# Moving the second tile of three pairs in the second DFT of an FNet block

## The chip, the cores and the metric

The kernel runs on one core of a Trainium2 chip. The metric is device time in microseconds (us) of one execution; lower is better. TensorE (PE) multiplies matrices into PSUM, VectorE (DVE) and ScalarE (ACT) do the elementwise work, GpSimd (POOL) a little of it, and SyncE (SP) issues all DMAs. Each engine runs its own instructions in the order in which they are written.

## The reference

```python
# x: 2048 x 448 (S x D), Df = 1792, all fp32
a = einsum("sd,ed->se", layernorm(x), dft_hid_re)
b = einsum("sd,ed->se", layernorm(x), dft_hid_im)
h = x + dft_seq_re @ a - dft_seq_im @ b            # FNet mixing
n = layernorm(h)
out = h + (gelu(n @ w_gate) * (n @ w_up)) @ w_down # GeGLU
```

## The kernel before, in words

Each fp32 operand is split into a high and a low fp16 part (`hi_part` on ACT, `lo_part` on DVE), and a product is three fp16 matmuls, so every tile of weights costs ACT and DVE work before PE can use it.

The kernel does the DFT along the sequence first, with x normalized ("first DFT", accumulators `acc` and `acc_f`), then the DFT along the hidden dimension (the "second DFT", accumulator `y`). After them comes the GeGLU in two parts (products `pX`, `pY`, `pZ`, then `acc_d`). The written order is the schedule: nothing reorders instructions, and code that is written later runs later on its engine.

The first DFT runs in 64 steps, n = 0 to 63 (`N_STEPS`). Steps 0 to 15 make the first four row tiles at once, steps 16 to 39 take 24 matmuls each, and from step 40 on (`FAST`) a Strassen scheme takes 42 narrower matmuls a step. Four such steps make a quad (40 to 43, 44 to 47 and so on), which shares four PSUM banks and ends with `fast_out`: DVE adds up the seven products (`e`) and splits the result into `zs`.

A Strassen step n needs "unit" n: the raw matrix `wr` (two DMAs, L421), its sums (`fast_sums`, DVE, L460 to L462), the high parts (ACT, L108: raw 128x768, sums twice 128x512) and the low parts (DVE, L114: 128x768 and 128x1024). From unit 43 on, a unit is written two steps before its use: unit 46 in step 44, 47 in 45, 48 in 46; units 45 and 49 stand between the matmuls of steps 43 and 47, together with `fast_out`. Three units fit in the ring `ws`, so ACT can start a unit when PE is done with the one three steps earlier. The load of `wr` for unit n can start when the low part of unit n-3's raw matrix is done.

Two row tiles (g = 0 and 1) make a pair p. For each pair, SP transposes `zs` into `z` (`z_turn`, L658, four DMAs; `z` has one buffer). For each tile of the pair, `hid_seed` (ACT, L700) puts x into the bank `y`, `hid_mm` adds 21 matmuls (PE, L719), and `hid_out` (ACT, L708 to L710) writes h and its moments from the bank. The bank `y` has a single buffer (tag `tr`), so the second tile's seed is written right behind the first tile's `hid_out`. `h_store` (SP, L733) writes the pair's h to memory; `ffn_rstd` makes the reciprocal deviation (one ACT instruction, L129, and five small DVE instructions, L140 to L144).

Two tables place this work: `early` (written after the units of step n) and `after` (written after the first or the second half of step n's matmuls, `(n, 0)` or `(n, 1)`). The first tile of pairs 0 to 6 stands at `(m, 0)`:

```python
m = (19, 24, 29, 36, 44, 52, 60)[p]
```

The fourth to sixth pair are p = 3, 4 and 5. In steps 42 to 44, ACT and DVE also normalize and split the h of p = 3 for the GeGLU (`xn_h`, `tt`, `xs`; `ffn_norm_act`, `ffn_sums`, `ffn_split`); the split stands in step 44 ahead of the `hid_out` of p = 4's first tile.

Of the kernel before, what the change touches and what calls it, by code (L numbers as in the profile page):

```python
# [32 lines left out]
def kernel(  # L33
# [92 lines left out]
    def root(mv, tag, of=1.0):  # L126
        n = mv.shape[1]
        sd = small.tile([P, n], F32, tag=f"sd{n}", name=f"sd_{tag}")
        A.activation(sd, mv[:, :, 1], AF.Sqrt, scale=1.0 / (of * X_SC**2), bias=eps_t)  # L129
        return sd  # L130
# [5 lines left out]
    def rstd(mv, sd, tag, pool=small, of=1.0):  # L136

        n = sd.shape[1]
        r = pool.tile([P, 4, n], F32, tag=f"r{n}" if pool is small else f"r_{tag}", name=f"r_{tag}")
        V.reciprocal(r[:, 0], sd)  # L140
        V.tensor_scalar(r[:, 1], mv[:, :, 1], of * EPS, -0.5 / (of * X_SC**2), op0=ALU.add, op1=ALU.mult)
        V.tensor_mul(r[:, 2], r[:, 0], r[:, 0])
        V.tensor_mul(r[:, 2], r[:, 2], r[:, 1])
        V.scalar_tensor_tensor(r[:, 3], r[:, 2], 1.5, r[:, 0], op0=ALU.add, op1=ALU.mult)  # L144
        return r[:, 3]
# [22 lines left out]
    def pair_tile(name, k):  # L168
        return ring.tile([P, 2, D], F32, tag=f"xh{k}", bufs=1, name=name)
# [28 lines left out]
    def ffn_rstd(q, j):  # L198
        tag = f"h{q}_{j}"
        mv = moments[q, j]  # L200
        moments[q, j] = mv, rstd(mv, root(mv, tag, D), tag, const, D)
# [18 lines left out]
    def ffn_bias(q, j):  # L220
        mv, r = moments[q, j]
        sign = -1.0 if (q, j) == (NB - 1, 1) else 1.0
        V.scalar_tensor_tensor(mv[:, :, 1], mv[:, :, 0], sign, r, op0=ALU.mult, op1=ALU.mult)

    def ffn_norm_act(q, j, h):

        tag = f"h{q}_{j}"
        mv, r = moments.pop((q, j))
        nb = mv[:, :, 1]
        xn = fops.tile([P, 2, D], F32, tag="xn", name=f"xn_{tag}")  # L230
        for g in range(2):
            A.activation(xn[:, g, :], h[:, g, :], AF.Identity, scale=r[:, g : g + 1], bias=nb[:, g : g + 1])
        ffn[q, j] = xn

    def ffn_sums(q, j, parts=range(4)):

        if 0 in parts:
            t = fops.tile([P, 960], F32, tag="tt", name=f"tt_{q}_{j}")
            ffn[q, j] = ffn[q, j], t
        xn, t = ffn[q, j][:2]  # L240
        sub = V.tensor_sub
        if 0 in parts:
            sub(t[:, 0:256], xn[:, 1, 0:256], xn[:, 0, 0:256])
        if 1 in parts:
            sub(t[:, 256:448], xn[:, 1, 256:448], t[:, 0:192])
            V.tensor_scalar(t[:, 448:512], t[:, 192:256], -1.0, None, op0=ALU.mult)
        if 2 in parts:
            sub(t[:, 512:704], xn[:, 1, 256:448], xn[:, 1, 0:192])
            V.tensor_scalar(t[:, 704:768], xn[:, 1, 192:256], -1.0, None, op0=ALU.mult)
        if 3 in parts:  # L250

            sub(t[:, 768:960], xn[:, 0, 256:448], t[:, 256:448])
# [31 lines left out]
    def ffn_split(q, j):  # L284
        ffn_hi(q, j)
        ffn_lo(q, j)

    def ffn_transpose(q, j, parts):
        xs = ffn[q, j][2]
        ops = hops[q if q > 1 else 0]  # L290
        c = (2 * q + j if q < 2 else j) * P
        for n in parts:
            s0, s1 = ((0, 8), (8, 16), (16, 22), (22, 25))[n]
            nc.sync.dma_start_transpose(ops[:, s0:s1, c : c + P], xs[:, s0 * P : s1 * P])
# [110 lines left out]
    N_STEPS = NT + 8 * (NP - 2)  # L405
    wr, ws = {}, {}

    def step_of(n):

        k, qq = divmod(n - NT, 4)  # L410
        return 2 + k // 2, k % 2, qq
# [242 lines left out]
    def z_turn(p):  # L654
        z[p] = hidp.tile([P, 2, 7, 2 * P], F16, tag="z", name=f"z{p}")
        for g in range(2):
            for l in range(2):
                nc.sync.dma_start_transpose(z[p][:, l, :, g * P : (g + 1) * P], zs[p][:, g, l, :])  # L658
# [32 lines left out]
    def h_tile(q, j):  # L691
        hp[q, j] = pair_tile(f"hx{q}_{j}", 2 * (q - 2) + j if q > 1 else j)
        nc.sync.dma_start(hp[q, j], xr[q // 2, 2 * (q % 2) + j])
# [3 lines left out]
    def hid_seed(p, g):  # L697

        y = ys[p, g] = ps_tr.tile([P, 512], F32, tag="tr", name=f"y_{p}_{g}")
        A.activation(y[:, :D], hp[p // 2, p % 2][:, g, :], AF.Copy, scale=D_SC)  # L700

    def hid_out(p, g):

        q, j = divmod(p, 2)
        if g == 0:
            moments[q, j] = const.tile([P, 2, 2], F32, tag=f"mv_h{q}_{j}", name=f"mv_h{q}_{j}")
        y, h, mv = ys[p, g][:, :D], hp[q, j][:, g, :], moments[q, j]
        A.activation(h, y, AF.Copy, scale=1.0 / D_SC, accum_out=mv[:, g, 0:1])  # L708
        A.activation(mv[:, g, 0:1], mv[:, g, 0:1], AF.Copy, scale=-1.0 / D)
        A.activation(y, y, AF.Square, scale=1.0 / D_SC, bias=mv[:, g, 0:1], accum_out=mv[:, g, 1:2])  # L710

    def hid_mm(p, g):

        if p == NP - 1:
            ys[p, g] = bank_tile("a3" if g else "tr", f"y_{p}_{g}")
        y = ys[p, g]
        for k in range(7):
            for m, (lz, lw) in enumerate(((0, 0), (0, 1), (1, 0))):
                PE.matmul(  # L719
                    y[:, :D],  # L720
                    z[p][:, lz, k, g * P : (g + 1) * P],
                    wh[:, lw, k, :],
                    start=p == NP - 1 and k == 0 and m == 0,
                    stop=k == 6 and m == 2,
                    skip_group_check=True,
                )
# [5 lines left out]
    def h_store(q, j):  # L732
        nc.sync.dma_start(h_dram[2 * q + j], hp[q, j])  # L733
# [6 lines left out]
    early, after = {}, {}  # L740

    def at(where, n, *what):
        where.setdefault(n, []).extend(what)
# [22 lines left out]
    for p, (n, half) in enumerate(turns):  # L766
        b, j = divmod(p, 2)
        m = (19, 24, 29, 36, 44, 52, 60)[p]
        at(early, m - 4, lambda b=b, j=j: h_tile(b, j))
        at(early, m - 2, lambda p=p: hid_seed(p, 0))  # L770
        for g in range(2):

            at(after, (m + g, int(p >= 3 and g)), lambda p=p, g=g: hid_mm(p, g), lambda p=p, g=g: hid_out(p, g))
            if g == 0:
                at(after, (m, 0), lambda p=p: hid_seed(p, 1))
        at(after, (n, half), lambda p=p: z_turn(p))
        at(early, m + 2 if p < 5 else N_STEPS - 7 + p, lambda b=b, j=j: ffn_rstd(b, j))
        at(after, (m + 2, 0), lambda b=b, j=j: h_store(b, j))
        if b < 2:

            m += 4 if p == 3 else 0
            at(early, m + 2, lambda b=b, j=j: ffn_bias(b, j), lambda b=b, j=j: ffn_norm_act(b, j, hp[b, j]))
            at(early, m + 3, lambda b=b, j=j: ffn_sums(b, j))
            at(early, m + 4, lambda b=b, j=j: ffn_split(b, j))
            for k in range(4):
                at(after, (m + 5 + k // 2, k % 2), lambda b=b, j=j, k=k: ffn_transpose(b, j, (k,)))
# [46 lines left out]
    for n in range(N_STEPS):  # L833
# [41 lines left out]
        if n >= FAST:  # L875

            last = n % 4 == 3
# [34 lines left out]
        else:  # L912
            p, part, qq = step_of(n)
# [381 lines left out]
    def bank_tile(tag, name):  # L1295
        return ps_ff[tag].tile([P, 512], F32, tag=tag, name=name)
# [102 lines left out]
    for t in range(NF, N_GU):  # L1399
# [37 lines left out]
        if ends:  # L1437
            p = now[-1] // NC
# [61 lines left out]
    for k in range(7):  # L1500
        for n in range(4, NC):
            dn_mm(7 * NC + n, range(3 * k, 3 * k + 3))
        for m, dst, sign in users.get(k, ()):
            h, ps = drain.x[dst], acc_d[7, "sums"][m][0]
            V.scalar_tensor_tensor(h, ps, sign * drain.sc, h, op0=ALU.mult, op1=ALU.add)
            if (m, dst) in ((2, 2), (3, 1), (5, 0), (6, 3)):
                g, c = divmod(dst, 2)
# [61 lines left out]
```

## Time and profile before

| | |
|---|---|
| median of 3 runs | 709.6 us (708.67 to 710.24) |
| the profiled execution: time, span | 706.87 us, 705.0 us |
| granted TensorE clock | 1.000 |
| PE busy | 696.2 us, 99% of the span |
| DVE busy, ACT busy | 551.3 us (78%), 400.2 us (57%) |

Times in the views are counted from the span's start. PE's ends are modelled, so its gaps are read from its list of waits, and from the starts of its instructions. Step 40 of the first DFT starts at 219.5 us, step 63 ends at 343.6 us.

### The profile page before, as it was taken

Reading aid. Unit: us, or ns where it says so; the run is one execution under the profiler, and the core shown is the slowest. Engines: PE = TensorE matmul, PEld = TensorE weight load, DVE = VectorE, ACT = ScalarE, POOL = GpSimd, SP = SyncE. Lnnn points to the kernel's source line nnn. Section 1 sums busy time; section 2 is a strip of 40 time slices with the busy share of each in tenths; the row PEclk is TensorE's granted clock in tenths of the full one; section 3 lists DMA queues with packets and bytes.
Section 4 is the critical chain, followed back from the end, with each engine's and each line's share of the span. In section 5 each row is a group of like instructions: output and inputs, shape, how many; then the busy total and the mean of one; then the engine's idle time right before and its main releaser. Section 6 shows DMA issues by size and latency. Waiting matters only on the chain.

```text
span 705.0 us, 13644 instructions
## 1 busy us (share of the span) xinstructions
PE 696.2 (99%) x5164; PEld 500.1 (71%) x5164; DVE 551.3 (78%) x1187; ACT 400.2 (57%) x787; POOL 95.5 (14%) x88
## 2 busy tenths in 40 slices
PE   8999999999999989999999999999999999999998
PEld 5555555555557869798744444469999999999997
DVE  7998667686878989798447798767777876899786
ACT  5876557666657565555536566545555453555531
POOL 0000000000000000000133333311020111232224
DMA  8798678999995568366845879797798985887612
GB/s 274 246 252 295 138 261 230 327 293 298 266 272 170 165 163 198 118 155 216 227 169 180 279 252 233 211 310 222 255 224 310 260 279 179 303 286 270 244 45 79
DMA packets 116321, 161.29 MB, mean 229 GB/s; under 512 B 61984, under 2 KB 80544, under 8 KB 116256
## 3 DMA queue, kind: packets, MB, share of 16 engines
q1 hardware_dynamic: 116256, 160.43, 75.8%
q8 instruction: 40, 0.66, 0.4%
q14 instruction: 25, 0.20, 0.1%
HBM read 112.16 MB, written 34.34 MB: 208 GB/s over the span
## 4 chain that ended last, share of the span: by engine, by line
PE 92%; DVE 3%; issue 2%; ACT 1%; DMA 1%; SPq 0%; DVEq 0%; ACTq 0%
PE acc L637 25%; PE acc_d L1229 15%; PE pY L1025 15%; PE acc_f L509 10%; PE pZ L1025 9%; PE pX L1025 9%; PE y L719 8%; DVE ws L114 1%; DMA wr<-in_w_seq_dram 1%; DMA x<-in_x_dram 0%; DVE sums L460 0%; ACT ws L108 0%; ACT xs L108 0%; DVE e L538 0%; DVE sums L461 0%
## 5 line engine op out<-in xcount | busy, mean ns | idle before, releaser
L637 PE MATMUL acc<-xs,ws 128*128 128x448 f16 x960 | 183.2, 352 | 0.7 <-DVE xs L149 0.7
L1025 PEld LDWEIGHTS <-gw 128*128 128x128 f16 x1443 | 140.9, 98 | 51.6
L637 PEld LDWEIGHTS <-ws 128*128 128x128 f16 x960 | 93.9, 98 | 88.4 <-ACT ws L108 0.6
L1229 PE MATMUL acc_d<-wd,dn_w 128*128 128x224 f16 x1008 | 110.6, 259 | 0.0
L1229 PEld LDWEIGHTS <-dn_w 128*128 128x128 f16 x1008 | 96.9, 98 | 1.9
L1025 PE MATMUL pY<-hops,gw 128*128 128x256 f16 (+1 forms) x629 | 98.1, 298 | 0.0
L509 PEld LDWEIGHTS <-ws 128*128 128x128 f16 x1008 | 96.6, 98 | 1.3
L114 DVE SCALAR_TENSOR_TENSOR ws<-wr,ws 128x1024 f16<-128x1024 f32 (+2 forms) x66 | 72.0, 1093 | 30.2 <-ACT ws L108 24.9
L1119 POOL TENSOR_TENSOR hs<-hs,c 128x256 f32<-128x256 f32 (+1 forms) x42 | 60.1, 1430 | 247.5 <-ACT c L1117 185.5
L719 PE MATMUL y<-wh,z 128*128 128x448 f16 x336 | 66.2, 352 | 3.4 <-ACT y L700 3.4
L509 PE MATMUL acc_f<-t,ws 128*128 128x224 f16 x576 | 68.3, 259 | 0.0
L108 ACT ACTIVATE ws<-wr 128x1024 f16<-128x1024 f32 (+2 forms) x66 | 62.0, 942 | 9.8 <-DMA wr<-in_w_seq_dram 8.3
L1025 PE MATMUL pX<-hops,gw 128*128 128x256 f16 (+1 forms) x407 | 67.1, 298 | 0.0
L1025 PE MATMUL pZ<-hops,gw 128*128 128x256 f16 (+1 forms) x407 | 67.1, 298 | 0.0
L719 PEld LDWEIGHTS <-z 128*128 128x128 f16 x336 | 32.9, 98 | 33.4 <-issue 3.6
L215 POOL TENSOR_TENSOR wd_s<-wd 128x448 f32<-128x448 f32 x7 | 10.0, 1427 | 341.0 <-DVE e L538 340.2
L1070 ACT ACTIVATE pY<-pX 128x256 f32<-128x256 f32 (+1 forms) x42 | 18.4, 439 | 66.2 <-PE pX L1025 65.8
L509 PE MATMUL acc_f<-xs,ws 128*128 128x224 f16 x432 | 54.8, 259 | 0.0
L1035 DVE SCALAR_TENSOR_TENSOR c<-pZ,u 128x256 f32<-128x256 f32 (+1 forms) x42 | 21.4, 511 | 39.4 <-PE pZ L1025 22.7
L1081 ACT ACTIVATE u<-pY 128x256 f32<-128x256 f32 (+1 forms) x42 | 19.1, 455 | 53.5 <-PE pY L1025 53.4
L112 DVE TENSOR_TENSOR dn_w<-dn_s,dn_w 128x640 f16<-128x640 f32 x48 | 41.6, 867 | 1.5 <-ACT dn_w L108 1.4
L108 ACT ACTIVATE dn_w<-dn_s 128x640 f16<-128x640 f32 x48 | 35.0, 729 | 12.1 <-DVE dn_s L1191 12.0
(144 smaller groups left out, 909.5 us busy)
## 6 DMA issues: line engine op xcount, KB each, us to landing
gw<-w_dram SPq DMA_DIRECT2D x37, 896.0 KB, 6.5
wr<-in_w_seq_dram SPq DMA_DIRECT2D x100, 256.0 KB, 4.3
hid_dram<-hs SPq DMA_DIRECT2D x27, 512.0 KB, 5.8
hid<-hid_dram SPq DMA_DIRECT2D x54, 256.0 KB, 5.5
w_dram<-gu_w SPq DMA_DIRECT2D x14, 896.0 KB, 6.3
gu_raw<-in_w_gu_dram SPq DMA_DIRECT2D x28, 384.0 KB, 6.3
wr<-in_w_seq_dram SPq DMA_DIRECT2D x14, 512.0 KB, 5.2
x<-in_x_dram SPq DMA_DIRECT2D x16, 224.0 KB, 3.1
```

Source lines behind the costliest of these rows:

```text
L108: A.activation(dst, src, AF.Copy, scale=scale)
L112: V.tensor_sub(dst, src, hi)
L114: V.scalar_tensor_tensor(dst, src, scale, hi, op0=ALU.mult, op1=ALU.subtract)
L509: PE.matmul(fast_sum(n, k), fast_a(n, i, lw, a), fast_b(j, lx, b), start=j == 0 and m == 0 and k % 2 == 0, stop=j == NT // 2 - 1 and m == ...
L637: PE.matmul(acc[key][:, :D], w[:, lw, block * P : (block + 1) * P], xs[c][:, lx, :], start=c == 0 and m == 0, stop=c == NT - 1 and m == 2,)
L719: PE.matmul(y[:, :D], z[p][:, lz, k, g * P : (g + 1) * P], wh[:, lw, k, :], start=p == NP - 1 and k == 0 and m == 0, stop=k == 6 and m == ...
L1025: PE.matmul(ps, w[:, wl, wa + ws, :], ops[:, m + ms, :], start=first and n == 0, stop=last and n == len(terms) - 1, skip_group_check=True,)
L1035: V.scalar_tensor_tensor(dst, ps, SC, other, op0=ALU.mult, op1=ALU.add)
L1070: A.activation(self.Y, self.X, AF.Copy)
L1081: A.activation(self.u2, self.Y, AF.Copy, scale=SC)
L1119: G.tensor_mul(c22, c22, self.cols(self.c12))
L1229: PE.matmul(ps, w[:, la, a, :], wd[n][:, lb, b, :], start=n == 0 and m == 0 and opens, stop=n == NC - 1 and m == 2, skip_group_check=True,)
```

## The change

For each pair it sets the place of the second tile's `hid_mm` and `hid_out` by a table of its own. For p = 0, 1, 2 and 6 the places come out as before. For p = 3 it goes from (37, 1) to (38, 0), for p = 4 from (45, 1) to (48, 0), for p = 5 from (53, 1) to (56, 0). The first tiles and all seeds stay. `h_store` goes along: for p = 3, 4, 5 from steps 38, 46, 54 to 39, 49, 57. `ffn_rstd` goes from step 38 to 40 for p = 3 and from 46 to 50 for p = 4; for p = 5 it stays at 62. No instruction is added or removed.

```diff
         m = (19, 24, 29, 36, 44, 52, 60)[p]
+        last = ((20, 0), (25, 0), (30, 0), (38, 0), (48, 0), (56, 0), (61, 1))[p]
+        m1 = last[0] + 1
...
-            at(after, (m + g, int(p >= 3 and g)), lambda p=p, g=g: hid_mm(p, g), lambda p=p, g=g: hid_out(p, g))
+            place = last if g else (m, 0)
+            at(after, place, lambda p=p, g=g: hid_mm(p, g), lambda p=p, g=g: hid_out(p, g))
...
-        at(early, m + 2 if p < 5 else N_STEPS - 7 + p, lambda b=b, j=j: ffn_rstd(b, j))
-        at(after, (m + 2, 0), lambda b=b, j=j: h_store(b, j))
+        at(early, m1 + p // 3 if p < 5 else N_STEPS - 7 + p, lambda b=b, j=j: ffn_rstd(b, j))
+        at(after, (m1, 0), lambda b=b, j=j: h_store(b, j))
```

On PE, the second tile of p = 4 stood before behind step 45. Here are the rows where its matmuls (`y_4_1`, from `z4`) begin and, after "...", where they end; `ws45`, `ws46` and `ws48` are the units of those steps:

```order
L509 MATMUL acc_f44_3_2660<-t2_3_2134,ws45_0_2581 128x224
L719 LDWEIGHTS z4_2425 [waits DMAHW4_49]
L719 MATMUL y_4_1_2732<-wh_167,z4_2425 128x448 [waits Activation_49]
...
L719 MATMUL y_4_1_2732<-wh_167,z4_2425 128x448
L509 LDWEIGHTS ws46_0_2662
```

On PE after the change, it stands in the middle of step 48:

```order
L509 MATMUL acc_f48_0_2940<-xs3_305,ws48_0_2814 128x224
L719 LDWEIGHTS z4_2425 [waits DMAHW4_49]
L719 MATMUL y_4_1_2732<-wh_167,z4_2425 128x448
...
L719 MATMUL y_4_1_2732<-wh_167,z4_2425 128x448
L509 LDWEIGHTS ws48_0_2814
```

Step 46's matmuls now follow step 45's at once, and the first matmul of the tile no longer carries a wait of its own for ACT.

On ACT, around steps 37 to 39, the rows before read (`y_3_1` is the second tile of p = 3, `ws41` unit 41, `tx3` and `t2_3` operands of the Strassen scheme, `gu_w2` weights of the GeGLU):

```order
L700 ACTIVATE y_3_1_2214<-hx1_1_1978 128x448 [waits Activation_49]
L708 ACTIVATE hx1_1_1978,mv_h1_1_2210<-y_3_1_2214 128x448 [waits PE_49,Activation_49]
L709 ACTIVATE mv_h1_1_2210<-mv_h1_1_2210 128x1 [waits Activation_49]
L710 ACTIVATE y_3_1_2214,mv_h1_1_2210<-y_3_1_2214,mv_h1_1_2210 128x448 [waits Activation_49]
L108 ACTIVATE ws41_0_2286<-wr41_2156 128x768 [waits DMAHW3_49,DMAHW2_49]
L108 ACTIVATE ws41_1_2287<-sums41_2285 128x512 [waits DVE_49] x2
L108 ACTIVATE gu_w2_2299<-gu_raw2_2044 128x512 [waits DMAHW6_49]
```

On ACT after the change, the same stretch and the rows behind it:

```order
L700 ACTIVATE y_3_1_2214<-hx1_1_1978 128x448 [waits Activation_49]
L108 ACTIVATE ws41_0_2262<-wr41_2156 128x768 [waits DMAHW3_49,DMAHW2_49,PE_49]
L108 ACTIVATE ws41_1_2263<-sums41_2261 128x512 [waits DVE_49,PE_49]
L108 ACTIVATE ws41_1_2263<-sums41_2261 128x512 [waits DVE_49]
L108 ACTIVATE gu_w2_2275<-gu_raw2_2044 128x512 [waits DMAHW6_49]
L108 ACTIVATE gu_w2_2275<-gu_raw2_2044 128x256
L382 ACTIVATE tx3_0_2228<-tx3_0_2228,affine_166 128x448 [waits DMAHW7_49]
L382 ACTIVATE tx3_1_2229<-tx3_1_2229,affine_166 128x448 [waits DMAHW0_49]
L708 ACTIVATE hx1_1_1978,mv_h1_1_2210<-y_3_1_2214 128x448 [waits PE_49,Activation_49]
```

Unit 41, the weights and `tx3` have moved ahead of the `hid_out` that waits for PE.

On SP, the transposes of `zs5` for the next pair (`z5`) stand behind these rows before, the store of p = 4's h (`h_dram4`) among them:

```order
L294 DMA_TRANSPOSE hops0_159<-xs_1_1_2675 128x6x128 [waits DMAHW4_49]
L733 DMA h_dram4_141<-hx2_0_2401 128x896 [waits DMAHW5_49,Activation_49]
L294 DMA_TRANSPOSE hops0_159<-xs_1_1_2675 128x3x128 [waits DMAHW6_49]
L421 DMA wr51_2944<-in_w_seq_dram 128x512 [waits DMAHW7_49,DVE_49]
L658 DMA_TRANSPOSE z5_3014<-zs5_2606 128x7x128 [waits DMAHW4_49,PE_49,Activation_49]
```

On SP after the change, from those transposes on:

```order
L658 DMA_TRANSPOSE z5_3005<-zs5_2606 128x7x128 [waits DMAHW3_49,PE_49,Activation_49]
L658 DMA_TRANSPOSE z5_3005<-zs5_2606 128x7x128 [waits DMAHW4_49,DVE_49]
L658 DMA_TRANSPOSE z5_3005<-zs5_2606 128x7x128 [waits DMAHW5_49,Activation_49]
L658 DMA_TRANSPOSE z5_3005<-zs5_2606 128x7x128 [waits DMAHW6_49,DVE_49]
L421 DMA wr53_3042<-in_w_seq_dram 128x512 [waits DMAHW7_49,DVE_49]
L421 DMA wr53_3042<-in_w_seq_dram 128x512 [waits DMAHW0_49]
L733 DMA h_dram4_141<-hx2_0_2401 128x896 [waits DMAHW1_49,Activation_49]
```

The store has moved behind the loads of unit 53, and the transposes' wait for PE, since `z` has one buffer, is now for matmuls that stand right ahead of them in step 48.

## The prediction

> **What bounds the kernel now.** I read the engines' busy shares first, then PE's list of waits, then the chain around its longest one, and last the engines at that place. On the page, PE is busy nearly throughout:
>
> ```profile
> PE 696.2 (99%) x5164; PEld 500.1 (71%) x5164; DVE 551.3 (78%) x1187; ACT 400.2 (57%) x787; POOL 95.5 (14%) x88
> ```
>
> PE's own waits of over half a us (us in total, times, longest) are few:
>
> ```profile
> PE y L719 <- ACT y L700: 3.4, 1, 3.4
> PE pw L102 <- POOL sign_t L93: 1.4, 1, 1.4
> PE acc L637 <- DVE xs L149: 0.7, 1, 0.7
> ```
>
> After the start, one wait of 3.4 us is all that PE has to lose to another engine: a second-DFT matmul waits for a seed. The chain of work that ended last shows where (start, us, what):
>
> ```profile
> 247.36 1.80 ACT xs L108 x4
> 249.16 0.53 ACT hx L708 x2
> ...
> 250.70 0.56 ACT y L700
> 251.26 0.04 issue
> 251.30 4.13 PE y L719 x21
> 255.44 26.16 PE acc_f L509 x273
> 281.60 3.97 PE y L719 x21
> 285.57 6.04 PE acc_f L509 x63
> 291.61 3.97 PE y L719 x21
> ```
>
> This is p = 4. Its first tile had its matmuls done by 241.8, but ACT came to that tile's output at 249.16 only, behind the split `xs` of p = 3; the seed of the second tile followed at 250.70 and PE went on at 251.30. From there to the end of the first DFT, PE stands in the chain without a gap. The rows of PE itself:
>
> ```profile
> 206.41 4.13 PE L719 MATMUL y<-wh,z 128*128 128x448 f16 x21
> 210.39 9.24 PE L637 MATMUL acc<-xs,ws 128*128 128x448 f16 x48
> ...
> 237.71 4.13 PE L719 MATMUL y<-wh,z 128*128 128x448 f16 x21
> ...
> 251.30 4.13 PE L719 MATMUL y<-wh,z 128*128 128x448 f16 x21 [3.42 <-ACT y L700]
> ```
>
> So PE is free at 251.30 - 3.42 = 247.88. Why was ACT late? Because of a wait of its own, at the second tile of p = 3 (ACT, then DVE; in brackets the idle time before a row and what ended it):
>
> ```profile
> 204.60 0.55 ACT L700 ACTIVATE y<-hx 128x448 f32<-128x448 f32 x1
> 210.65 0.55 ACT L708 ACTIVATE hx<-y 128x448 f32<-128x448 f32 x1 [5.50 <-PE y L719]
> ...
> 212.17 0.83 ACT L108 ACTIVATE ws<-wr 128x768 f16<-128x768 f32 x1
> ...
> 214.97 1.40 ACT L382 ACTIVATE tx<-tx,affine 128x448 f32<-128x448 f32 x2
> 217.73 0.58 ACT L108 ACTIVATE t<-tx 128x448 f16<-128x448 f32 x1 [1.36 <-DVE tx L572]
> ```
>
> ```profile
> 207.21 0.42 DVE L462 TENSOR_TENSOR sums<-wr,sums 128x256 f32<-128x256 f32 x1
> 213.04 0.96 DVE L114 SCALAR_TENSOR_TENSOR ws<-wr,ws 128x768 f16<-128x768 f32 x1 [5.40 <-ACT ws L108]
> ...
> 216.16 0.16 DVE L140 RECIPROCAL r_h<-sd_h 128x2 f32<-128x2 f32 x1
> ...
> 216.82 0.39 DVE L571 TENSOR_TENSOR tx<-tx 128x224 f32<-128x224 f32 x1
> ...
> 219.80 0.68 DVE L460 TENSOR_TENSOR sums<-wr 128x512 f32<-128x512 f32 x1
> ```
>
> ACT stood for 5.50 us on PE's matmuls at 206.41, with the ready unit 41 queued behind it, and DVE stood 5.40 us behind ACT. Then DVE hardly rests again: by stretches (us, PE, PEld, DVE, ACT, POOL busy, clock, DMA share, GB/s),
>
> ```profile
> 235.60:251.30 15.70, 12.28 (x107) 10.07 (x105) 14.62 (x34) 10.80 (x23) 0.00 (x0) 1.00 0.39 136
> ...
> 307.50:323.60 16.10, 16.10 (x160) 15.16 (x158) 15.75 (x27) 8.25 (x15) 0.00 (x0) 1.00 0.76 187
> ```
>
> DVE is busy 14.62 of the 15.70 us that end in PE's wait, and 15.75 of 16.10 in a quad without second-DFT work. A quad of PE costs as much as its DVE work, so each 4 us of second DFT is DVE's only time to catch up.
>
> **The change, part by part.** *The wait.* With the second tile of p = 4 in step 48, PE goes from step 45 into step 46 at 247.88. A step takes 26.16 / 6.5 = 4.02 us (273 matmuls at 42 a step) and a tile 3.97, so steps 46, 47 and 48 start at 247.9, 251.9 and 255.9, the tile at 257.9, and the second half of step 48 at 261.9. Before, that half came at 251.30 + 4.13 + 2.5 x 4.02 = 265.5: 3.4 us of gain, if the units are there. The seed is then ready 7 us ahead.
>
> *The cover that is gone.* Before, the wait and the tile hid the preparation of units 46 to 48 (DVE; the last row is unit 54's):
>
> ```profile
> 247.58 1.22 DVE L114 SCALAR_TENSOR_TENSOR ws<-sums,ws 128x1024 f16<-128x1024 f32 x1
> ...
> 250.79 0.68 DVE L460 TENSOR_TENSOR sums<-wr 128x512 f32<-128x512 f32 x1
> ...
> 252.31 0.95 DVE L114 SCALAR_TENSOR_TENSOR ws<-wr,ws 128x768 f16<-128x768 f32 x1
> 253.18 1.22 DVE L114 SCALAR_TENSOR_TENSOR ws<-sums,ws 128x1024 f16<-128x1024 f32 x1
> 254.31 0.69 DVE L460 TENSOR_TENSOR sums<-wr 128x512 f32<-128x512 f32 x1
> ...
> 257.93 0.96 DVE L114 SCALAR_TENSOR_TENSOR ws<-wr,ws 128x768 f16<-128x768 f32 x1 [2.01 <-ACT ws L108]
> ...
> 260.77 0.69 DVE L460 TENSOR_TENSOR sums<-wr 128x512 f32<-128x512 f32 x1
> ...
> 288.03 1.22 DVE L114 SCALAR_TENSOR_TENSOR ws<-sums,ws 128x1024 f16<-128x1024 f32 x1
> ```
>
> At these times unit 46 is ready at 248.80, but step 46 wants its sums after six matmuls, at 248.45: 0.35 late. Unit 47's raw part is ready at 253.26; step 47, by then at 252.25, loses 1.0. Unit 48 no longer has `hid_out` ahead of it, so its raw part follows its sums at 254.31 + 1.6 and is done by 256.9, its sums by 258.1, against 257.3 and 257.9: 0.2 late. That sums to 1.6 lost, a gain of 1.8.
>
> *The second tile of p = 3.* But that tile moves too, behind half of step 38: its matmuls run 206.41 + 2.3 (12 of the 48 matmuls in 9.24 us) = 208.7 to 212.65. ACT no longer stands at them with unit 41 behind: unit 41's sums were done at 207.63, so its high parts, before at 212.17, run from 205.2 and 207.6 on. The weights and `tx3` (before at 214.97) follow, then `hid_out`, whose wait now ends at 212.75 and which takes the 1.52 us of the rows 210.65 to 212.17. At 214.3, ACT makes the high parts of `tx3`, which before began at 217.73: a lead of 3.4 us, and DVE's sums of unit 42 come at 216.4 in place of 219.80. The five instructions of `ffn_rstd` (216.16 to 216.82, 0.7 with its last one) now stand ahead of unit 43 and give back that much: 2.7 us of lead. I find nothing that takes it before step 46. PE's place is the same up to 247.88, DVE is busy nearly all of 219.8 to 249, and what it waits for (PE's steps 39 to 43, the loads of `wr`) is there about 2 us or more ahead of the new, earlier need. The nearest is unit 45's load, behind p = 4's transposes, which wait for DVE's `zs` and so move up along with it:
>
> ```profile
> 225.06 6.87 SPq L658 DMA_TRANSPOSE z<-zs  x4
> ...
> 266.78 5.40 SPq L658 DMA_TRANSPOSE z<-zs  x4
> 272.27 20.32 SPq L421 DMA_DIRECT2D wr<-in_w_seq_dram  x12
> ```
>
> With 2.7 us of lead, unit 46 is there at 246.1 (wanted 248.45), unit 47's raw part at 250.6 (251.9), unit 48's at 254.2 or sooner (255.9). No wait is left. I take this end, 3.4, and keep 1.8 as the other.
>
> *Behind it.* Unit 49's sums came at 260.77 behind p = 4's `ffn_rstd`, which now stands in step 50; they come at 251.6 + 3.8 (unit 48's sums and low parts) = 255.4, a lead of 5.3 us against PE's 3.4. *The queue of SP:* p = 4's store moves behind unit 53's loads and nothing waits for it. The transposes into `z` now wait for the tile of p = 4, done at 261.9; their `zs` is done at about 262, so they start when their data are there, some 5 us sooner than at 266.78, and unit 53's loads follow. Nothing. *The tile of p = 5* moves from 291.61 to behind half of step 56. Units 54 to 56 lose 4 us of cover. Unit 54 was ready at 289.25; with DVE 4.6 us ahead (5.3, less the moved `ffn_rstd`) it is at 284.7, and the next two follow at DVE's 3.5 us a unit (sums of 47 at 250.79, of 48 at 254.31), at 288 and 292. PE wants them at 288, 292 and 296. Nothing, and ACT's `hid_out` of that tile no longer blocks unit 56. Everything after step 63 starts 3.4 us earlier in the same order.
>
> **The sum.** -3.4 us. The profiled execution took 706.87 (span 705.0), so it would take 703.4. The median of the runs shown is 709.6, 2.7 above it; the same 3.4 from it gives 706.2.
>
> At one place a page of the Trainium skill reads otherwise. The rows first: the 21 matmuls take 4.13 us behind the gap as at 206.41 and 237.71, and the clock in the stretches is 1.00. "TensorE: Matmul & The Clock Gate", in "Part 1: The HAM clock gate", says that TensorE's clock falls to half after an idle window of about 3.4 us, counted on a free-running window, and stays there for as long. The gap of 3.42 us is just that long, so by the page some executions may lose another 1.7 us behind it, which would go too: an estimate of 704.5. The profiled execution doesn't show it.
>
> **The rivals.** *Half the gain:* the lead of p = 3 doesn't reach step 46, because another wait takes it. For it speaks how busy DVE is; against it that each wait I find ends earlier as well. Then 1.8: 707.8.
>
> *More than the gap:* the runs shown lie 1.8 to 3.4 above the profiled one; if this excess comes from slower matmuls behind the gap, up to 2.7 more goes. At half of that, 704.8. The rows show no slow matmul.
>
> *Nothing:* PE's gap only moves, to step 47 or 48, or to the weights of the GeGLU: 709.6. For it speaks that DVE works as long per quad as PE; against it the 1 us and more that each unit has to spare.
>
> *Slower:* ACT's late `hid_out` of p = 3 (212.75 in place of 210.65) becomes a lag and not a lead, if `tx3`, now ahead of it, lands late and holds ACT. Steps 46 to 48 then stand bare in front of DVE. The gain is used up when unit 47's raw part ends 2 us later than the 253.26 of before (251.9 + 3.4), and the kernel is 1.4 slower or worse past 256.7: 711.0 and up. At such a lag of 3.4, `t` starts at 217.73 + 3.4 = 221.1; less 1.52 for `hid_out` and 1.40 for `tx3`, its load would have to land after 218. Before, ACT took it at 214.97 without a wait.
>
> **How the numbers follow.** 0.2% is 1.4 us, about what a measurement tells from no change. The whole gap, 706.2: 0.66, with 705.3 to 707.1 as its own range by the spread of the runs. Half the gain, 707.8: 0.14. More, 704.8: 0.07. Nothing, 709.6: 0.08. Slower: 0.05. The range from 704.7 to 708.6 holds the first two and half of the third. Faster takes the first, the third and about half of the second: 0.8; same 0.14; slower 0.06.
>
> **What would show it.** PE's list of waits loses its first line, and has none at L509 of over 0.5 us; a wait for DVE's `ws` there is the second case. ACT's wait of 5.5 us at 210.65 falls to some 2 us, DVE's of 5.4 likewise, and the sums of unit 42 come near 216.4. Step 63 ends near 340.2. I am wrong if those sums don't move up, or if PE reaches the GeGLU no earlier.

## The result, and the profile after

The change takes the kernel from 708.92 us to 703.37 us (medians), a ratio of 0.9921 with a 95% interval of 0.9908 to 0.9934: 5.5 us faster. Forecast were 3.4 us and 706.2, with a range from 704.7 to 708.6. The direction held, and the gap went as forecast; the gain is 2 us larger than the one term that was summed. The profiled executions alone (spans 705.0 before and 701.1 after) differ by 3.9 us, 0.2 of it an earlier start: step 40 begins at 219.24 in place of 219.47. After the change the mean granted clock is 0.999 or 1.000 in each of the six runs.

The page after, PE's busy time and PE's list of waits:

```profile
PE 696.3 (99%) x5164; PEld 500.6 (71%) x5164; DVE 551.0 (79%) x1187; ACT 400.0 (57%) x787; POOL 95.4 (14%) x88
```

```profile
PE pw L102 <- POOL sign_t L93: 1.4, 1, 1.4
PE acc_d L1232 <- ACT v L958: 0.2, 1, 0.2
```

The wait for the seed is gone, and no wait for a unit (L509) has come in its place. In the chain, PE runs through the whole stretch (start, us, what):

```profile
237.51 3.97 PE y L719 x21
241.49 16.10 PE acc_f L509 x168
257.59 3.97 PE y L719 x21
261.56 16.10 PE acc_f L509 x168
277.66 3.97 PE y L719 x21
281.63 16.10 PE acc_f L509 x168
297.73 3.97 PE y L719 x21
...
331.79 8.05 PE acc_f L509 x84
```

168 matmuls are four steps of 42 with no gap between them. The second tile of p = 4 starts at 257.59 (forecast 257.9), the first Strassen phase ends at 339.84 (forecast 340.2, before 343.77 in the chain). ACT and DVE after, in the order of the forecast's steps:

```profile
212.69 0.55 ACT L708 ACTIVATE hx<-y 128x448 f32<-128x448 f32 x1 [0.76 <-PE y L719]
...
247.60 0.55 ACT L700 ACTIVATE y<-hx 128x448 f32<-128x448 f32 x1
```

```profile
215.89 0.68 DVE L460 TENSOR_TENSOR sums<-wr 128x512 f32<-128x512 f32 x1
...
244.47 1.22 DVE L114 SCALAR_TENSOR_TENSOR ws<-sums,ws 128x1024 f16<-128x1024 f32 x1
...
249.20 0.95 DVE L114 SCALAR_TENSOR_TENSOR ws<-wr,ws 128x768 f16<-128x768 f32 x1
...
252.72 0.95 DVE L114 SCALAR_TENSOR_TENSOR ws<-wr,ws 128x768 f16<-128x768 f32 x1
```

ACT's wait of 5.50 us is 0.76 (some 2 us were forecast), and DVE's of 5.40 is gone, with two shorter ones, 1.01 and 1.60 us, in its place. The sums of unit 42 come at 215.89 (forecast 216.4), unit 46 is ready at 245.7, unit 47's raw part at 250.2, unit 48's at 253.7: each a little ahead of the forecast and of PE.

### The profile page after: what moved, and what is told of

Same layout as the page of the kernel before. It is cut to its first block, busy times and chain, and to the rows that moved or that the text cites. A ratio compares the mean times of both kernels' runs of the same rounds, so it can differ in the third digit from the quotient of the medians.

```text
span 701.1 us, 13638 instructions
## 1 busy us (share of the span) xinstructions
PE 696.3 (99%) x5164; PEld 500.6 (71%) x5164; DVE 551.0 (79%) x1187; ACT 400.0 (57%) x787; POOL 95.4 (14%) x88
## 4 chain that ended last, share of the span: by engine, by line
PE 98%; issue 1%; DMA 0%; DVE 0%; ACT 0%
PE acc L637 26%; PE acc_d L1232 15%; PE pY L1028 15%; PE acc_f L509 14%; PE pZ L1028 10%; PE pX L1028 10%; PE y L719 9%; DMA x<-in_x_dram 0%; ACT dn_w L108 0%; ACT v L958 0%; DVE st_x L122 0%; DVE xs L149 0%; DVE hr L1508 0%; ACT sd_x L129 0%; DVE r_x L373 0%
## 5 line engine op out<-in xcount | busy, mean ns | idle before, releaser
L509 PEld LDWEIGHTS <-ws 128*128 128x128 f16 x1008 | 96.6, 98 | 1.3
L509 PE MATMUL acc_f<-t,ws 128*128 128x224 f16 x576 | 68.2, 259 | 0.0
L509 PE MATMUL acc_f<-xs,ws 128*128 128x224 f16 x432 | 55.1, 259 | 0.0
```

Source lines behind the costliest of these rows:

```text
L509: PE.matmul(fast_sum(n, k), fast_a(n, i, lw, a), fast_b(j, lx, b), start=j == 0 and m == 0 and k % 2 == 0, stop=j == NT // 2 - 1 and m == ...
```

## The experiments

After the result the question was where the other 2 us came from. Three theories were held against each other. A is the clock: TensorE runs at less than its full clock behind the gap in most executions (the rival "more than the gap"). B is a gap that is usually longer than in the trace shown. C is another place.

**The kernel before, unchanged** (run `same`): no edit.

> The kernel before, unchanged, to see its usual executions (span and clock of each) and a second trace. The profiled execution of before took 706.87 us, its other runs 708.42 to 710.24; the change gained 5.55 us by the runs but 3.67 by the profiled executions. Theory A, clock: in most executions PE runs slow for some us behind the 3.4 us gap, so their spans are some 707 us with a mean clock of 0.998 to 0.999, and a trace with such a span shows a clock under 1 in the stretch from 251 us on. Theory B, longer gap: the spans are as long, the clock is 1.000, and the wait for the seed is some 5.5 us. Theory C, elsewhere: the gap is 3.4 us and the excess lies in another place of the trace.

Measured: 709.0 us against 709.03, ratio 0.9998 (0.9990 to 1.0007). Its trace has a span of 707.8 and a mean clock of 0.995. PE around the gap:

```profile
237.49 4.13 PE L719 MATMUL y<-wh,z 128*128 128x448 f16 x21
251.13 7.09 PE L719 MATMUL y<-wh,z 128*128 128x448 f16 x21 [3.48 <-ACT y L700]
```

The gap is the same 3.48 us, but the 21 matmuls behind it take 7.09 us in place of 4.13. By stretches, the column after POOL is the granted clock:

```profile
251.30:253.00 1.70, 1.70 (x6) 0.66 (x5) 1.63 (x4) 1.59 (x3) 0.00 (x0) 0.50 1.02 195
253.00:255.00 2.00, 2.00 (x7) 0.86 (x6) 1.97 (x4) 0.00 (x0) 0.00 (x0) 0.50 0.80 174
255.00:257.00 2.00, 2.00 (x7) 0.76 (x5) 0.71 (x2) 0.00 (x0) 0.00 (x0) 0.50 1.04 259
257.00:259.00 2.00, 2.00 (x16) 1.49 (x15) 0.00 (x0) 0.66 (x3) 0.00 (x0) 0.96 0.00 1
```

PE works all of these 7.7 us and gets half of its clock up to about 257.1. This is theory A, with a lower mean clock than the 0.998 to 0.999 that was expected. B falls (3.48 us), and so does C: the slow matmuls lose 2.96 us, and this execution's span is 2.8 us over the 705.0 of the other trace. In 47 executions of before's code (11 of this run, 36 beside it and beside the later runs), the mean clock and the median time go together: clock 0.998, 12 executions, 708.3 us; 0.997, 26, 708.9; 0.995, 8, 709.7; and one at 1.000 with 707.1. The trace of `same` is of the slowest kind; the usual execution, at 0.997, loses 1.8 us against the one at full clock. The profiled execution that the forecast was made from, with its clock of 1.000 and 706.87, was of the rare kind at 1.000.

**Only p = 4 moves** (run `p4_only`):

```diff
-            at(after, (m + g, int(p >= 3 and g)), ...)
+            place = (48, 0) if (p, g) == (4, 1) else (m + g, int(p >= 3 and g))
+            at(after, place, ...)
```

with its `ffn_rstd` and `h_store` as in the change.

> Only the second tile of p = 4 moves, to step 48; p = 3 and p = 5 stand as before. By the prediction's step on the cover that is gone, PE waits 0.35, 1.0 and 0.2 us for units 46 to 48 and 1.8 of 3.4 us are gained: a span of 703.2 against 705.0. Rival: the waits don't come and the span is 701.6. By the runs, A adds its 2 us of slow clock to the gain, since no gap of 3.4 us is left (3.9 in all, some 705.0 us); B and C give 1.8 (707.1).

Measured: 704.67 us, ratio 0.9935 (0.9923 to 0.9948); span 702.9, clock 1.000. PE, at the start of step 47:

```profile
253.29 1.13 PE L509 MATMUL acc_f<-xs,ws 128*128 128x224 f16 x10 [0.84 <-DVE ws L114]
```

DVE's raw part of unit 47 ends at 253.23, as in the kernel before, and PE waits for it: the prediction's 1.0 us for unit 47 is there, its 0.35 and 0.2 for the others are not to be seen. The runs are 1.3 us above the full change, of which this wait explains 0.84; the rest is open. So the cover mattered, and p = 3's lead is what pays for it. A's 705.0 is nearer than 707.1.

**Only p = 3 moves** (run `p3_only`):

```diff
+            place = (38, 0) if (p, g) == (3, 1) else (m + g, int(p >= 3 and g))
+            at(after, place, ...)
```

with its `ffn_rstd` in step 40 and its `h_store` in step 39.

> Only the second tile of p = 3 moves, to step 38; the second tile of p = 4 stays behind step 45. The trace of the change shows p = 4's seed done at 248.15 where before it was done at 251.25, so the gap shrinks from 3.4 to some 0.4 us: a gain of 3.0 in the span (702.0). Rival: without the move of p = 4 the lead is lost before step 45 and the gap stays over 2 us. By the runs, A adds 2 us (gain 5, 703.9), B and C give 3.0 (705.9).

Measured: 704.40 us, ratio 0.9933 (0.9919 to 0.9947); span 702.6, clock 1.000. PE at p = 4's second tile, behind step 45:

```profile
248.90 4.13 PE L719 MATMUL y<-wh,z 128*128 128x448 f16 x21 [1.04 <-ACT y L700]
```

The gap shrinks to 1.04 us (0.4 was expected; the seed is done at 248.85, 0.7 later than in the change's trace), and the matmuls behind it take their 4.13. The time is 1.03 us above the full change: about the gap. Each of the two moves alone thus gives most of the gain, since each alone brings the gap far below 3.4 us.

**Another way to shorten the gap** (run `split_late`): no tile is moved; the split of p = 3's h stands one step later on ACT and DVE.

```diff
-            at(early, m + 4, lambda b=b, j=j: ffn_split(b, j))
+            at(early, m + 4 + (p == 3), lambda b=b, j=j: ffn_split(b, j))
```

> The kernel before with one other edit: the split of p = 3's h stands in step 45, one step later, so ACT's 1.7 us of it no longer stand ahead of p = 4's first output and second seed. No tile is moved. The gap shrinks from 3.4 to 1.7 us. A: a gap of 1.7 us slows no clock, so the runs gain 1.7 + 2 = 3.7 us (705.2). B and C: 1.7 (707.2). Rival for the cause of the gap: if it isn't ACT's queue, the gap stays and nothing is gained.

Measured: 705.42 us, ratio 0.9947 (0.9935 to 0.9960); span 703.6, clock 1.000.

```profile
249.84 4.13 PE L719 MATMUL y<-wh,z 128*128 128x448 f16 x21 [1.60 <-ACT y L700]
```

The gap is 1.60: without the split's 1.8 us ahead of it in ACT's queue, the seed comes that much sooner. The gain of 3.6 us is twice the 1.8 by which the gap shrank, as A expects (705.2).

**The gap filled, not removed** (run `busy_gap`):

```diff
+    def busy():
+        t = ps_seq.tile([P, 512], F32, tag="mm", name="busy")
+        for k in range(18):
+            PE.matmul(t[:, :D], fast_w[45][0][:, 0, :P], xs[0][:, 0, :], start=k == 0, stop=k == 17)
...
+            if g and p == 4:
+                at(after, (m + 1, 1), busy)
```

> The kernel before, with 18 useless matmuls of 128x448 (0.19 us each, 3.4 in all, into a free PSUM bank that nothing reads) ahead of the second tile of p = 4, so that PE works while it would wait for the seed. No useful work starts sooner. A (the clock falls because PE idles): the wait falls under 0.2 us, the tile still starts at 251.3, the clock is 1.000, the span some 705.0 and the runs 706.9, 2.1 under before. If the clock falls for another reason at this place (load, a transfer), the runs stay at 709.0 with a clock of 0.997. B and C: 709.0 as well.

Measured: 706.91 us against 708.52, ratio 0.9977 (0.9968 to 0.9986); span 705.4, clock 1.000.

```profile
247.82 3.57 PE L769 MATMUL busy<-xs,ws 128*128 128x448 f16 x18
251.68 4.13 PE L719 MATMUL y<-wh,z 128*128 128x448 f16 x21 [0.29 <-ACT y L700]
```

This separates the two terms. The second tile starts no sooner than before (251.68), no useful work is saved, and yet the kernel is 1.6 us faster: its matmuls take 4.13 us, at the full clock. ACT's, DVE's and the DMAs' work at the place is the same, so PE's idling is the cause. From here to the full change it is 3.5 us, the gap.

**A gap of 2.7 us** (run `gap_26`): `split_late` with this ahead of p = 4's second seed:

```diff
+            if g == 0 and p == 4:
+                at(after, (m, 0), *[lambda: A.activation(warm, eps_t, AF.Copy)] * 5)
```

> The split of p = 3 in step 45 (as in the run split_late, gap 1.6 us) and five tiny ACT copies of 128x1 into an unused tile (0.22 us each) ahead of p = 4's second seed, so the gap is about 2.7 us. If the clock falls whenever PE has idled some 2.4 us (in the second trace of before it fell at 250.3, 2.4 us behind the gap's start), the clock is 0.997 and the runs some 708.5. If it needs an idle stretch of 3.4 us, the clock is 1.000 and the runs are 705.4 + 1.1 = 706.5.

Measured: 707.45 us, ratio 0.9987 (0.9978 to 0.9996), span 705.8, clock 0.997; of ten executions three had a clock of 1.000, with 706.6 to 707.1 us, the others (0.997 or 0.998) 707.3 to 708.6.

```profile
250.45 5.81 PE L719 MATMUL y<-wh,z 128*128 128x448 f16 x21 [2.74 <-ACT y L700]
```

A gap of 2.74 us is enough, in most executions, to cost another 1.68 us. Neither expectation fits wholly: the median lies between them, since both kinds of execution occur.

**A longer gap** (run `gap_55`): the kernel before with ten such copies.

> The kernel before and ten tiny ACT copies ahead of p = 4's second seed: the gap grows from 3.4 to some 5.6 us. With A the clock falls in every execution, and the runs are 709.0 + 2.2 and up to 1 more, since the executions of before that lost least (clock 0.998) now lose as much as the others: 711.2 to 712.2.

Measured: 710.95 us, ratio 1.0037 (1.0023 to 1.0050); span 708.7, and a clock of 0.995 in each execution.

```profile
252.59 6.51 PE L719 MATMUL y<-wh,z 128*128 128x448 f16 x21 [5.08 <-ACT y L700]
```

The gap is 5.08 us (5.6 was expected). The matmuls behind it lose 2.4 us; part of the slow stretch lies in the gap itself, where it costs nothing. The time is just below the 711.2 expected.

**Without the move of p = 5** (run `p3_p4`): in the changed kernel,

```diff
-        last = (..., (38, 0), (48, 0), (56, 0), (61, 1))[p]
+        last = (..., (38, 0), (48, 0), (53, 1), (61, 1))[p]
```

> The changed kernel with the second tile of p = 5 back behind step 53 (place (53, 1)); p = 3 and p = 4 stand as in the change. The prediction has the move of p = 5 at nothing: the same 703.4 us. Rival: PE or ACT meets a wait there (before, ACT stood 3.87 us for that tile with unit 56 behind it), and it is 0.5 to 2 us slower.

Measured: 703.48 us, ratio 0.9931 (0.9918 to 0.9943), span 701.1, clock 1.000. The same as the change: the move of p = 5 gives nothing, as forecast.

Put together, by the longest gap in the trace and the median time:

| run | gap, us | time, us | time less 703.4 and the gap |
|---|---|---|---|
| the change | 0 | 703.37 | 0.0 |
| p4_only | 0.84 | 704.67 | 0.4 |
| p3_only | 1.04 | 704.40 | 0.0 |
| split_late | 1.60 | 705.42 | 0.4 |
| gap_26 | 2.74 | 707.45 | 1.3 |
| before | 3.4 to 3.5 | 708.5 to 709.0 | 1.7 to 2.1 |
| gap_55 | 5.08 | 710.95 | 2.5 |

Up to 1.6 us, a gap costs about what it is long (within 0.4 us); from 2.7 us on, PE's slow clock behind it costs 1.3 to 2.5 us more.

## Why the prediction was wrong

The step that failed is the sum: "-3.4 us", its only term, taken from the profiled execution and carried over to the median as if the two differed by nothing that the change touches. They did: before, the median of six runs stands 2.05 us above the profiled execution (708.92 and 706.87), after only 0.17 (703.37 and 703.20). The term that the sum left out is the matmuls at half clock behind the gap, which go with the gap.

The prediction had this term in hand. It wrote that slower matmuls behind the gap could be the reason for the excess of the median, and gave that case 0.07 and 704.8 us, because "The rows show no slow matmul". They showed none because that one execution had none; 46 of the 47 others have a mean clock of 0.998 or less. The term was weighed by a sample of one.

What the runs put in its place: 1.6 us by `busy_gap` (1.0 to 2.3 by its interval), 1.8 by before's executions at 0.997 against the one at 1.000, 2.0 by what is left of the change's 5.5 less 3.5. So 706.2 was 2.8 us too high: some 2.1 is this term, and 0.7 is that the median of before, 709.6 by three runs, is 708.92 by six.

The page of the Trainium skill named in the prediction, "TensorE: Matmul & The Clock Gate" ("Part 1: The HAM clock gate"), led to an estimate of 1.7 us and 704.5: nearer than the rows did. With the rows of `same`, `gap_26` and `gap_55` the trace agrees that the clock falls to just half, and for some 3.4 us (251.0 to 254.5 in `gap_26`) or twice that (250.3 to 257.1 in `same`). It doesn't agree that a wholly idle window of 3.4 us is needed: 2.74 us of idling did it in seven of ten executions.

Point by point, the rest held. *The wait:* 3.42 us, gone; PE reaches the end of the first DFT 3.93 us sooner in the chain (339.84 against 343.77), 0.2 of it by the earlier start. *The cover that is gone:* without p = 3's lead, 1.6 us of waits were forecast for units 46 to 48, and `p4_only` shows 0.84 as a wait and 1.3 in the time. *The lead of p = 3:* 3.4 us forecast at unit 42, 3.9 measured (215.89 against 219.80), 2.7 forecast at units 46 to 48, 3.1 measured (245.69 against 248.80 for unit 46); 0.2 of each is the earlier start. *The queue of SP*, from its list after:

```profile
261.62 5.25 SPq L658 DMA_TRANSPOSE z<-zs  x4
266.96 1.21 SPq L421 DMA_DIRECT2D wr<-in_w_seq_dram  x2
268.27 0.38 SPq L733 DMA_DIRECT2D h_dram<-hx  x1
```

The transposes start 5.2 us sooner than before ("some 5 us"), with unit 53's load and the store right behind. *p = 5:* nothing, shown by `p3_p4`. *Slower:* the load of `tx3` did hold ACT for 0.65 us, and the weights ahead of it for 0.87, inside the time it would have waited for PE; no lag came of it. *Half the gain* and *nothing* did not happen.

## What to carry to other kernels

Before an execution's trace is taken as the kernel, hold its time and its mean clock against the other runs: a median that lies 2 us above the profile is a term of the sum that has to be found, not an offset to be carried along. Here gaps in PE of 2.7 to 5.1 us cost some one and a half times their length, since matmuls behind them ran at half clock; by the table, gaps up to 1.6 us didn't, and useless matmuls in the gap of 3.4 us won 1.6 us. When an in-order engine reaches a piece of work late, look for the earlier wait that made it late: here moving either of two tiles, or one split, took away the same gap or more than half of it.

## What the runs showed of the hardware

The clock falls with a delay. In `same` PE idled from 247.65 and the clock fell at about 250.3; in `gap_55` it idled from 247.51 and the clock fell at about 250.6; in `gap_26` PE idled from 247.71, worked again from 250.45, and the clock fell at about 251.0, when PE was busy again. Here are the stretches of `gap_26` in which it fell and came back, and the one of `same` in which it fell (the granted clock stands after POOL again):

```profile
250.00:251.00 1.00, 0.55 (x3) 0.29 (x3) 0.28 (x1) 1.00 (x2) 0.00 (x0) 1.00 0.36 127
251.00:252.00 1.00, 1.00 (x4) 0.40 (x3) 0.81 (x1) 1.00 (x3) 0.00 (x0) 0.52 0.00 0
...
254.00:255.00 1.00, 1.00 (x6) 0.48 (x5) 1.00 (x3) 0.00 (x0) 0.00 (x0) 0.77 0.00 0
```

```profile
250.00:250.50 0.50, 0.00 (x0) 0.00 (x0) 0.50 (x4) 0.50 (x2) 0.00 (x0) 0.82 0.41 152
```

So most of the loss lies behind the gap and not in it, and how long the clock stays low differs. In `gap_26`, where PE was at work all the while, the clock came back after 3.4 us. In `same` and `gap_55`, where PE came back only 0.8 and 2.0 us after the fall, it came back after 6.8 us. The same gap thus loses different amounts: in 47 executions with gaps in the same place, mean clocks of 0.995, 0.997, 0.998 and 1.000 were seen. A mean clock of 0.995 over 707 us is worth 3.5 us of full clock, 0.998 is worth 1.4. What decides which of them an execution gets was not tried.
